# A written work list that reaches to the end of the first FFN group

## The chip, the cores and the metric

The program runs on one core of one Trainium2 chip. The metric is the time of one execution on the device in microseconds (us). The engines in this text are PE (TensorE, matrix products), DVE (VectorE), ACT (ScalarE), POOL (GpSimd) and SP (it issues most transfers). Each engine works through its own queue in order; a row that waits holds up all rows behind it on that engine.

## The reference

```python
# attention: 4 batches, 8 heads, 768 tokens, head size 64; 4 sink keys, window 128
scores = q @ k.T / sqrt(64); keep = is_sink | in_window
a = softmax(where(keep, scores, -1e9)); x = a @ v      # heads side by side: 4 x 768 x 512
# Fourier mix
u = x + real(fft(fft(x, axis=1), axis=2))
# FFN with a normalised input
un = (u - mean(u)) / sqrt(var(u) + 1e-6)
out = u + relu(un @ w_ch1) @ w_ch2                     # 512 -> 2048 -> 512
```

## The kernel before

The 3072 tokens are 24 blocks of 128. The attention walks over them block by block: scores into a double-buffered PSUM tile `s` (L843), a merge and a maximum on DVE (L858, L872), the exponentials on ACT (L883), transposes `pt` (L908), the products with the values `xt` (L944), a transpose back with the sink part added, `x` (L956, L958), and the division on DVE into `us` or `u` (L973). The Fourier mix of a batch, products with constant matrices in two stages (L444, then L471 and L493), runs beside the attention of the next batch; its DVE part splits sums into a high and a low half (L426, L456, L458), combines (L498, L499) and adds into `u` (L509, L510).

The FFN works on six groups of four blocks. Every operand is a pair, a high half rounded by ACT and a low half (a difference) by DVE or POOL, and a product is three products of halves. For an inner tile `f` of 128 columns (sixteen of them), `ch1` (L701, twelve matmuls of 512 columns) makes `h`, `relu` (L749, ACT) the high half, `relu_lo` (L754, DVE) the low half, and `ch2` (L761, twelve matmuls) adds into four accumulators `o`. In the text `h(f)` and `o(f)` are these two sets of twelve matmuls in the first group. The weights arrive as 64-bit pairs of words: three DVE rows join them (L654 to L656, a "join"; number `2f` is the first weight of tile `f`, `2f+1` the second), ACT makes the high half (L684), POOL the low half (L691).

The second group needs, before its first product, for its four blocks: statistics on DVE (L563, L564), a chain of fourteen small DVE steps on a 128x4 tile (L570 to L579), a scaled row block `un` (L587, DVE), four transposes `unt` (L593, PE), and two halves `un_last` (L597 ACT, L602 DVE).

What sets the order: everything up to tile 9 of the first group is called from one string, `WORK`, a letter per call; each letter takes the next call of its kind. This stretch is under the manual schedule, so each engine's queue has the calls in the order of the string. Tiles 10 to 15 of the first group and the second group's preparation (`prepare(1)`) follow in ordinary code without that schedule. There the framework places the rows by its own priorities, and it may put them among the rows of the string where their inputs exist. From the second group on, a loop under the manual schedule sets the order.

```python
for c in WORK or plain:
    other_bank[0] = c
    next(todo[OTHER.get(c, c)])()
```

Of the kernel before, what the change touches and what calls it, by code (L numbers as in the profile page):

```python
# [11 lines left out]
F32 = mybir.dt.float32  # L12
F32R = mybir.dt.float32r
# [6 lines left out]
P = 128  # L20
B, H, S, D = 4, 8, 768, 64
# [32 lines left out]
PREP_N = 4  # L54
# [88 lines left out]
}  # L143
OTHER = {"R": "r", "X": "T", "Y": "T"}
WORK = (
    "TskTsTvqTqTTMTTTTTTTTTTTTTCMfefVsefetifmscvewfqmetiafcRfeswftyViemsvvcGaefwqftemiscoRfeGdtfwyxVmsciq"
    "ueoffweaVzoetmiARscfGnyadewfVoemtivxsVqcufewfeVmiaoetzfRiscVGdyahfweVmtoxvsfcvfuqewdeiamSoetziRfacfy"
    "ewslktoxefufGcsVvqiaezAwfteVoRacdyeswftxViemSuocfsivefawVeqGztmRaciSVyswSxftedGufcmGaesvvfBtwfeqVosc"
    "VaeitzxwmRuycoaVGafedifBTwmeosvqVxitfaVcGfermsnyewztfoucdieafGmseqwvtfBofeVisczTxwmeorufyAidteafcmse"
    "wvqtZhofiTfczewTmeorsfkyiaAleXZxdfTeffTiAdeTZedtuicAswvqzaZofTGeVTftAVXcZGerswydaAoBmitfxTfcewuAsevS"  # L150
    "zTVGqmaDtifTHcfeVrXwyAaeVsHSDxtdTicmHuAfTefwzteosDvvGcaVqirBsmytwfoafcTVHxmeuefsqwVteofaezimsGncahfH"
    "fermvsywxqHteLucfaefotziemsGcaiBLwVrovTyxfdXwAfeTmoeitZisLvqcTAwfefomTeZtiALafudcfeswkzreoLayZisqxvL"
    "TfeLfLdeTLltiALXcZwTLfotAfaeLZTeLdLuLcdiLTwzrsyALoVtGamTcfTfxwtVeuLGeLsvSaAiBzqmTGcVrNwysSCDtfHefTma"
    "eHTfcVsixvteVvwqaOcaAfroqqqqqqemuwTyzoxsfieDtGVHTcTfuemaAwLBToVsGtDafcVieTfvzxHermsNywfedotfaCGmcsie"
    "OHaLBwuvVxtoTcfeHafAzsemNiwfrCdoyfetiOsvcmuewZotLTicfeTfwzeoramyiANfxZtCdacf0OeTwdeoWTiYATZEXdAIWTtA"
    "TcawrZETZYoAWuITyxTAaDEazWIuxTTVEYAPIDVHTVSJSTYAHPzDVVBKuVJVVz1V2VBKVVV2VBVVTVV3jjWYAZAHETZWIYAZEWTA"
    "IPAZEZWITJYAKETWAPIDEVTJIYAKTDPVHAWH2WEITJ2DEKVI2WPHEWI4JKEW2IWEPIWEIPJWEIKE2WJIKEPWIWE2JIKEWIPWEI2J"
    "KEWIWEIEI"
)
# [81 lines left out]
def kernel(  # L241
# [55 lines left out]
    def run(general):  # L297
        tag = "g" if general else ""
        with ExitStack() as p1:
# [463 lines left out]
            def window_attention(fourier, clear, load_constants):  # L763
                with ExitStack() as pa:
# [216 lines left out]
                    with ExitStack() as man:  # L981
# [194 lines left out]
                        def first_group(s):  # L1176
# [9 lines left out]
                            def fourth():  # L1186
                                pf.close()
                                state["pw"] = p1.enter_context(tc.tile_pool(name="wb" + tag, bufs=1))

                            yield s, "second", second  # L1190
                            for f in range(F_LIST):
                                if f > 1:
                                    yield s, "P", lambda f=f: first_product(f)

                                def relu_hi(f=f):
# [4 lines left out]
                                for _ in range(PER_F):  # L1200
# [3 lines left out]
                                    s += 1  # L1204
                                if f < 2 or f > 2:
# [6 lines left out]
                                for i in () if f < 1 else range(4, 8) if f == 1 else range(2 * f + 4, 2 * f + 6):  # L1212
                                    if i == NWA:
# [217 lines left out]
            pw = state.get("pw")  # L1431
            un_last = []
            with (tc.manual_schedule() if MAN0 else ExitStack()):
# [390 lines left out]
```

## Time and profile before

| | |
|---|---|
| median of 3 runs | 742.84 us (741.91 to 743.32) |
| the profiled execution | 742.85 us |
| its span in the trace | 741.1 us |
| PE busy | 721.6 us, 97% of the span |
| DVE busy | 598.8 us, 81% |
| ACT, POOL busy | 344.4 and 180.6 us |

The first product of the second group starts at 303.40 us; the written list covers roughly the first 270 us. A row of the timeline gives start and duration of a piece; square brackets give the idle time of the engine ahead of it and what ended it. Matmuls overlap, so the pitch of a row of them is read from one start to the next.

### The profile page before, as it was taken

To read this page: it belongs to the slowest core of one execution; us is meant where nothing else is said; L and a number is where in the kernel's file an instruction comes from. 1 tells how busy PE (TensorE), PEld (TensorE's weight loads), DVE (VectorE), ACT (ScalarE), POOL (GpSimd) and SP (SyncE) were. 2 spreads that over 40 slices of the span, in tenths; PEclk is the share of its full clock that TensorE was granted. 3 is DMA by queue.
4 is the path that set the end of the run, shared out by engine and by line. 5 is a ranking of instruction groups with operands and counts; after the bars stand their busy time and mean duration, and the time that the engine had idled before them with its cause. 6 is when DMAs were issued, how large, how long until landed. Compare 5 with 4: busy or idle time off the path is not lost.

```text
span 741.1 us, 14738 instructions
## 1 busy us (share of the span) xinstructions
PE 721.6 (97%) x5223; PEld 622.2 (84%) x5223; DVE 598.8 (81%) x1630; ACT 344.4 (46%) x896; POOL 180.6 (24%) x289
## 2 busy tenths in 40 slices
PE   8999999999999999999999999999999999999995
PEld 6677878878787788798988989898989898989895
DVE  7999799899999999597778889587877889564445
ACT  5998678676332333344553333333334233423330
POOL 3686585785344544000000000000000000000002
PEclk9999999999999999999999999999999999999998
DMA  9976245334124653244466566755775657565751
GB/s 249 318 221 188 65 142 157 103 104 169 58 99 171 213 199 115 72 184 157 178 220 237 163 186 221 244 160 174 231 236 170 188 164 241 161 182 164 229 180 61
DMA packets 95306, 129.18 MB, mean 174 GB/s; under 512 B 5956, under 2 KB 60748, under 8 KB 94968
## 3 DMA queue, kind: packets, MB, share of 16 engines
q1 hardware_dynamic: 94216, 124.00, 52.4%
q0 software_dynamic: 720, 3.76, 1.5%
q8 instruction: 43, 0.70, 0.4%
q10 hardware_dynamic: 288, 0.39, 0.1%
q14 instruction: 39, 0.32, 0.1%
HBM read 104.00 MB, written 24.13 MB: 173 GB/s over the span
## 4 chain that ended last, share of the span: by engine, by line
PE 82%; DVE 11%; ACT 3%; issue 1%; DMA 1%; SPq 0%; POOL 0%; DVEq 0%; ACTq 0%
PE h L701 34%; PE p L1535 26%; PE xt L944 4%; PE o L761 4%; PE s L843 3%; PE pt L908 2%; ACT sm L883 1%; PE zb L444 1%; PE za L444 1%; PE x L956 1%; DVE sm L872 1%; PE a L471 1%; DVE s L858 1%; PE zr L444 1%; PE b L493 1%
## 5 line engine op out<-in xcount | busy, mean ns | idle before, releaser
L1535 PE MATMUL p<-w_ring,h_sums 128*128 128x256 f32 x936 | 131.4, 282 | 0.0
L1535 PEld LDWEIGHTS p<-w_ring,h_sums 128*128 128x128 f32 x936 | 123.0, 188 | 3.5 <-DVE u L1367 0.2
L1483 ACT CAST h_sums<-sums 128x256 fp32r<-128x256 f32 (+2 forms) x158 | 89.7, 568 | 68.4 <-PE p L1535 31.1
L1484 DVE TENSOR_TENSOR h_sums<-sums,h_sums 128x256 fp32r<-128x256 f32 (+2 forms) x158 | 98.2, 622 | 17.5 <-ACT h_sums L1483 16.4
L1535 PE MATMUL p<-w2t,h_sums 128*128 128x256 f32 x702 | 110.3, 282 | 0.0
L1557 POOL TENSOR_TENSOR u<-u,u 128x512 f32<-128x512 f32 x3 | 3.8, 1298 | 427.1 <-DVE u L1557 427.1
L1535 PEld LDWEIGHTS p<-w2t,h_sums 128*128 128x128 f32 x702 | 97.6, 189 | 3.4
L701 PE MATMUL h<-un_slots,w 128*128 128x512 f32 x396 | 97.8, 395 | 0.0
L701 PE MATMUL h<-un_last,w 128*128 128x512 f32 x396 | 97.1, 394 | 0.0
L701 PEld LDWEIGHTS h<-un_slots,w 128*128 128x128 f32 x396 | 72.5, 188 | 15.1
L701 PEld LDWEIGHTS h<-un_last,w 128*128 128x128 f32 x396 | 72.2, 188 | 15.0 <-DVE un_slots L602 0.7
L883 ACT ACTIVATE sm<-sm,mx 128x132 f32<-128x132 f32 x192 | 75.8, 399 | 5.1 <-DVE mx L872 4.9
L1697 ACT ACTIVATE sums<-h 128x512 f32<-128x512 f32 x40 | 23.9, 597 | 99.1 <-PE h L701 99.1
L1387 DVE STREAM_TRANSPOSE unf<-un 32x128 f32<-32x128 f32 x192 | 58.1, 302 | 2.8
L1494 DVE TENSOR_TENSOR sums<-sums 128x256 f32<-128x256 f32 x39 | 16.4, 421 | 48.5 <-ACT sums L1697 48.3
L1665 ACT ACTIVATE sums<-h 128x512 f32<-128x512 f32 x40 | 23.9, 598 | 67.7 <-PE h L701 67.7
L872 DVE CUSTOM_DVE_ANT_0 sm<-s,mask 128x132 f32<-128x132 f32 x192 | 45.9, 286 | 3.0 <-DVE s L858 0.5
L944 PE MATMUL xt<-ptl,ldv 128*64 128x128 f32 x384 | 38.0, 284 | 0.0
L843 PE MATMUL s<-ring,q 64*64 64x196 f32 (+1 forms) x640 | 36.3, 340 | 1.6 <-DVE mx L872 1.6
L924 POOL TENSOR_SCALAR_AFFINE_SELECT ptl<-pta 128x512 f32<-128x512 f32 x48 | 32.5, 678 | 19.9 <-ACT pta L915 19.2
L858 DVE COPY_PREDICATED s<-other,s 64x256 f32<-64x256 uint8 x80 | 34.4, 430 | 3.0 <-PE s L843 0.3
L883 ACT ACTIVATION_READ_ACCUMULATOR sm<-sm,mx 128x1 f32 x192 | 36.6, 191 | 0.0
(242 smaller groups left out, 1352.4 us busy)
## 6 DMA issues: line engine op xcount, KB each, us to landing
w_ring<-w2s SPq DMA_DIRECT2D x62, 512.0 KB, 4.4
w2t<-w2s SPq DMA_DIRECT2D x93, 256.0 KB, 3.2
raw<-in_moe_w_ch_dram SPq DMA_DIRECT2D x32, 512.0 KB, 3.2
w2s<-w_ring SPq DMA_DIRECT2D x16, 512.0 KB, 3.3
ldv<-in_v_dram SPq DMA_DIRECT2D x28, 256.0 KB, 2.9
ring<-in_qk_dram SPq DMA_DIRECT2D x24, 264.0 KB, 4.6
w2s<-w2t SPq DMA_DIRECT2D x24, 256.0 KB, 2.5
out_dram<-u SPq DMA_DIRECT2D x22, 256.0 KB, 4.8
```

The lines of the kernel that those rows point to most:

```text
L701: T.matmul(ps[:, :tb], a[:, cs], x[:, :, cc, :], start=n == 0, stop=n == 3 * NCC - 1)
L761: T.matmul(po[i], a[:, ts_], x, start=f == 0 and n == 0, stop=f == NF - 1 and n == 2)
L843: T.matmul(ps[HC * x:HC * x + HC, j, c:c + k.shape[-1]], st["q", g][rows, hp + i, HC * x:HC * x + HC], k, start=True, stop=True)
L858: V.copy_predicated(part(rows, c_out), other[qi > 2][rows], part(rows, c_in))
L872: V.tensor_tensor_reduce(sm[:, h % 4], ps[:, j, c:c + W], mask[min(qi, 3)], -SCALE, 3.0e38, ALU.add, ALU.min, accum_out=mx[:, 0, h:h + 1])
L883: A.activation(sm[:, h % 4], sm[:, h % 4], AF.Exp, bias=mx[:, 0, h:h + 1], scale=-1.0, accum_out=mx[:, 1, h:h + 1])
L924: G.affine_select(lo, a, [[0, 4], [s, P]], compare_op=ALU.is_ge, fill=0.0, base=0, channel_multiplier=-s)
L944: T.matmul(ps[D * j:D * j + D, p, :], st["v", kb(g) - i][:, h, :], a[:, h % 4, :], start=i == 0, stop=i == n - 1)
L1387: V.transpose(unf[32 * q:32 * q + 32, :, r], un[r].rearrange("p (c q j) -> p c q j", c=NCC, q=4)[:, :, q])
L1483: A.copy(hc_hi[:, left(a, n)], src)
L1484: V.tensor_tensor(hc_lo[:, left(a, n)], src, f32(hc_hi[:, left(a, n)]), op=ALU.subtract)
L1535: T.matmul(acc[i][:, 2 * P * tp:2 * P * tp + 2 * P], x, w, start=q == 0 and tp == 0 and n == 0, stop=q == end and n == 2, skip_group_check ...
```

## The change

`F_LIST` (10) goes. The string now also holds tiles 10 to 15 of the first group and the second group's statistics (`p`), scaled rows (`p`), transposes (`b`) and halves (`g`, `Q`), and the opening of the pool that they need (`fifth`). The ordinary loop is left for the general case alone. The string is a new one from its first letters on: rows of the attention and of the Fourier mix have changed places too. The rows themselves are the same on every engine; only their order differs.

```diff
-F_LIST = 10
+    0: "D", 1: "Z", ..., "fourth": "4", "fifth": "5", "p": "p", "b": "b", "g": "g", "Q": "Q", ...
 WORK = (
-    "TskTsTvqTqTTMTTTTTTTTTTTTTCMfefVsefetifmscvewfqmetiafcRfeswftyViemsvvcGaefwqftemiscoRfeGdtfwyxVmsciq"
...
-    "KEWIWEIEI"
+    "TskTTqsTvqTTMCTTTTTTTTTTTTTMfefVsefetifmsvcewfqfetiVsGcmRewafytiefamcsevvwftfeiqmsocRGfxdwyufeVmosqe"
...
+    "PEWpIp2WEJIKEPpWIpWE2IpWEI5PJKEpWIPJKEpWI2pWEIJ2pKEpIWbPgpEQIWbJPgKEQIp2WWEbJ2IgKEQIpPbJ2gKQ"
 )
...
+                            def fifth():
+                                state["pg"].close()
+                                wl = state["wl"] = p1.enter_context(tc.tile_pool(name="wl" + tag, bufs=1))
+                                un_last.append(wl.tile([P, 2, 2, NCC, 2 * P], F32R, name="un_last"))
+                                hc.append(wl.tile([P, 2, len(LEFT) * 2 * P], F32R, name="h_sums"))
+                                hc.append(wl.tile([P, 2, 2 * P], F32R, name="w2t3"))
+                                state[1] = [u_of(*x) for x in groups[1]], [un_last[0][:, :, i] for i in range(2)]
+
+                            def second_group():
+                                blocks = list(enumerate(groups[1]))
+                                for i, x in blocks:
+                                    yield "p", lambda i=i, x=x: stats(*x, u_of(*x), i, groups[1][0])
+                                dev = deviations(*groups[1][0], len(blocks))
+                                for _ in range(14):
+                                    yield "p", lambda: next(dev, None)
+                                for i, x in blocks:
+                                    yield "p", lambda x=x: un_make(*x, u_of(*x))
+                                    yield "b", lambda i=i, x=x: un_turn(*x, banks[1][0].tile([P, 512], F32, tag=banks[1][1], ...))
+                                    yield "g", lambda i=i, x=x: un_hi(*x, state[1][1], i)
+                                    yield "Q", lambda i=i, x=x: un_lo(*x, state[1][1], i)
...
-                            for f in range(F_LIST):
+                            for f in range(NF):
...
+                                if f == PREP:
+                                    yield s, "ch2", lambda: ch2(PREP - 1, hs.pop(PREP - 1), state["po"])
+                                    yield s, "fifth", fifth
...
+                                for _ in range(PREP_N * 2 if f >= PREP else 0):
+                                    x = next(more, None)
+                                    if x:
+                                        yield s, *x
...
-                for f in range(0 if general else F_LIST, NF):
+                for f in range(NF if general else 0):
```

Three places of the order. In the names, the number ahead of the last one is a block, a tile or a part; the last is a serial number that means nothing here.

First, PE where the attention ends. `x_3342` and `x_3332` are the last output block, `h_1` is the first product of tile 1, `o_0` the first accumulator, `ptah` and `ptlh` the halves of tile 0's `h`. Before:

```order
L493 MATMUL b_2_3307<-cst,zb_2_3170 128x258
L701 MATMUL h_1_3318<-un_slots,w_ring 128x512 x12
L956 MATMUL x_3342<-ident,xs_3250 128x128 x4
L958 MATMUL x_3342<-vs_1964,skt_3201 128x512
L761 MATMUL o_0_3362<-w_ring,ptah_3300 128x512 x2
L761 MATMUL o_0_3362<-w_ring,ptlh_3301 128x512
```

Now:

```order
L492 MATMUL b_2_3321<-cst,zb_2_3164 128x258
L959 MATMUL x_3332<-ident,xs_3317 128x128 x4
L961 MATMUL x_3332<-vs_1968,skt_3190 128x512
L700 MATMUL h_1_3341<-un_slots,w_ring 128x512 x12
L764 MATMUL o_0_3365<-w_ring,ptah_3289 128x512 x2
L764 MATMUL o_0_3365<-w_ring,ptlh_3290 128x512
```

The last output block now stands ahead of `h(1)` and no longer directly ahead of `o(0)`.

Second, DVE in the first tiles of the FFN. `stat` is the 128x4 tile of the second group's chain, `cv`, `cw` and `w2r` are what joins write, `zr` is a low half of the last Fourier mix. Before, at joins 5 and 6:

```order
L654 TENSOR_SCALAR w2r_3470<-raw_3189 128x512
L564 BN_AGGR stat_4_4040<-bn_1_4050 128x2
L655 SCALAR_TENSOR_TENSOR w2r_3470<-raw_3189,w2r_3470 128x512
L570 TENSOR_SCALAR stat_4_4040<-stat_4_4040 128x4
L656 SCALAR_TENSOR_TENSOR w2r_3470<-raw_3189,w2r_3470 128x512
L456 TENSOR_TENSOR zr<-zr_3_3458,zr 1x386
L654 TENSOR_SCALAR cv_3491<-raw_3241 128x512
L572 TENSOR_SCALAR stat_4_4040<-stat_4_4040 128x4
L655 SCALAR_TENSOR_TENSOR cv_3491<-raw_3241,cv_3491 128x512
```

Now the chain's first two steps stand here, at joins 14 and 15 and the low half of `h(6)`:

```order
L653 TENSOR_SCALAR cw_3800<-raw_3725 128x512
L654 SCALAR_TENSOR_TENSOR cw_3800<-raw_3725,cw_3800 128x512
L655 SCALAR_TENSOR_TENSOR cv_3799<-raw_3725,cw_3800 128x512
L569 TENSOR_SCALAR stat_4_2306<-stat_4_2306 128x4
L653 TENSOR_SCALAR cw_3823<-raw_3762 128x512
L654 SCALAR_TENSOR_TENSOR cw_3823<-raw_3762,cw_3823 128x512
L655 SCALAR_TENSOR_TENSOR w2r_3792<-raw_3762,cw_3823 128x512
L757 SCALAR_TENSOR_TENSOR h_0_6_3844<-h_6_3807,h_0_6_3843 128x512
L571 TENSOR_SCALAR stat_4_2306<-stat_4_2306 128x4
```

The chain's other twelve steps follow one by one between the joins up to number 27, and the first two scaled rows, which stood after the low half of `h(2)` and ahead of that of `h(5)`, now stand behind the low half of `h(12)` and behind join 28. On PE the first block's transposes, which stood between `h(5)` and `o(5)`, stand behind `o(11)`, so that `o(5)` follows `h(5)` directly; `h(12)` stands ahead of `o(10)`.

Third, PE in the attention, at the second score group of block 5 (`s_2_673`, `s_2_661`) and the transposes `pt_1` of block 4. Before:

```order
L944 MATMUL xt_600<-pta_3_516,ldv_293 64x128 x2
L908 MATMUL pt_1_663<-ident,sm_0_583 128x128 x4
L843 MATMUL s_2_673<-ring,q_391 64x196
L843 MATMUL s_2_673<-ring,q_391 64x200
L843 MATMUL s_2_673<-ring,q_391 64x196
```

Now:

```order
L947 MATMUL xt_623<-pta_3_534,ldv_291 64x128 x2
L846 MATMUL s_2_661<-ring,q_402 64x196
L846 MATMUL s_2_661<-ring,q_402 64x200
L846 MATMUL s_2_661<-ring,q_402 64x196
L846 MATMUL s_2_661<-ring,q_402 64x200
L846 MATMUL s_2_661<-ring,q_402 64x196
L846 MATMUL s_2_661<-ring,q_402 64x200
L846 MATMUL s_2_661<-ring,q_402 64x196
L846 MATMUL s_2_661<-ring,q_402 64x200
L911 MATMUL pt_1_676<-ident,sm_0_587 128x128 x4
```

The four transposes have moved behind the scores. Moves of this kind, by one or two rows, are found in most blocks.

## Rows read from the trace of the kernel before

**Rows 1.** The page, part 1: busy time of each engine, its share of the span, and its instructions.

```profile
PE 721.6 (97%) x5223; PEld 622.2 (84%) x5223; DVE 598.8 (81%) x1630; ACT 344.4 (46%) x896; POOL 180.6 (24%) x289
```

**Rows 2.** Stretches of the whole program: length, then busy time and instructions of PE, PEld (weight loads), DVE, ACT and POOL, the granted PE clock as a share of full speed, the share of the DMA engines, GB/s.

```profile
100.00:150.00 50.00, 49.98 (x572) 39.97 (x570) 46.13 (x188) 38.00 (x141) 36.18 (x67) 1.00 0.47 138
...
200.00:250.00 50.00, 45.80 (x222) 38.17 (x221) 48.50 (x89) 14.38 (x28) 21.68 (x18) 0.97 0.40 137
...
650.00:700.00 50.00, 50.00 (x314) 44.99 (x313) 25.86 (x49) 17.41 (x30) 0.00 (x0) 1.00 0.59 180
```

**Rows 3.** Timeline of PE from the end of the attention to the second group: start, duration, row, and in brackets the idle time ahead with what ended it. `unt` are the second group's transposes.

```profile
199.17 0.70 PE L761 MATMUL o<-w_ring,ptah 128*128 128x512 f32 x2 [1.26 <-DVE us L973]
...
209.26 0.62 PE L444 MATMUL zr<-cst,gh 128*128 128x386 f32 x2 [0.80 <-DVE za L458]
...
213.23 0.62 PE L444 MATMUL zb<-cst,gh 128*128 128x386 f32 x2 [0.36 <-DVE zr L456]
...
224.91 0.95 PE L471 MATMUL a<-cst,za 128*128 128x258 f32 x6 [1.73 <-DVE d L499]
...
239.21 2.89 PE L701 MATMUL h<-un_slots,w 128*128 128x512 f32 x12
241.94 0.60 PE L593 MATMUL unt<-ident,un 128*128 128x128 f32 x4
242.78 0.50 PE L761 MATMUL o<-w2t,h 128*128 128x512 f32 x1 [0.25 <-ACT h L749]
243.95 0.49 PE L761 MATMUL o<-w2t,h 128*128 128x512 f32 x1 [0.67 <-POOL w2t L691]
244.84 4.14 PE L761 MATMUL o<-w2t,h 128*128 128x512 f32 x10 [0.39 <-DVE h L754]
248.82 0.63 PE L701 MATMUL h<-un_slots,w_gh 128*128 128x512 f32 x2
...
254.32 2.90 PE L761 MATMUL o<-w_ring,h 128*128 128x512 f32 x12
257.06 0.62 PE L701 MATMUL h<-un_slots,w_gh 128*128 128x512 f32 x2
...
303.40 2.97 PE L701 MATMUL h<-un_last,w_ring 128*128 128x512 f32 x12
```

**Rows 4.** Stretches of 1 us around tile 5: length, PE busy time and instructions, the granted PE clock (1.00 is 2.4 GHz, 0.50 is 1.2 GHz), DMA.

```profile
245.00:246.00 1.00, 1.00 (x4) 0.60 0.63 254
246.00:247.00 1.00, 1.00 (x4) 0.50 0.00 0
247.00:248.00 1.00, 1.00 (x4) 0.50 0.00 0
248.00:249.00 1.00, 1.00 (x4) 0.69 0.87 287
```

**Rows 5.** Timeline of DVE in the same part: `bn` and `stat` are the second group's statistics and chain, `un` its scaled rows, `za` and `d` rows of the last Fourier mix, `h` and `h_sums` the low halves of `h(5)` and `h(10)`, `cv` the last row of join 14.

```profile
206.20 0.68 DVE L563 BATCH_NORM_STATS2 bn<-u 128x6 f32<-128x512 f32 x1
...
208.66 0.55 DVE L458 TENSOR_TENSOR za<-za,za 128x386 fp32r<-128x386 f32 x1
...
211.31 0.70 DVE L570 TENSOR_SCALAR stat<-stat 128x4 f32<-128x4 f32 x1
...
213.94 1.26 DVE L572 TENSOR_SCALAR stat<-stat 128x4 int32<-128x4 int32 x1
...
224.02 0.42 DVE L498 TENSOR_TENSOR d<-asb,b 128x257 f32<-128x257 f32 x1
...
242.69 1.49 DVE L587 TENSOR_SCALAR un<-u,stat 128x512 f32<-128x512 f32 x1
244.11 0.68 DVE L754 SCALAR_TENSOR_TENSOR h<-h,h 128x512 fp32r<-128x512 f32 x1
...
248.62 0.69 DVE L656 SCALAR_TENSOR_TENSOR cv<-raw,cw 128x512 int32<-128x512 int32 x1
...
274.56 0.69 DVE L754 SCALAR_TENSOR_TENSOR h_sums<-h,h_sums 128x512 fp32r<-128x512 f32 x1 [1.08 <-ACT h_sums L749]
```

**Rows 6.** DVE rows that read or write `stat` (chain, aggregates, scaled rows) in two stretches: length, busy time and instructions.

```profile
205.00:246.00 41.00, 7.05 (x18) 0.99 0.45 154
246.00:304.00 58.00, 2.00 (x2) 0.98 0.46 155
```

**Rows 7.** Timeline of ACT: the high half of `h(5)` and that of join 14.

```profile
242.13 0.60 ACT L749 ACTIVATE h<-h 128x512 fp32r<-128x512 f32 x1 [1.49 <-PE h L701]
...
249.34 0.62 ACT L684 CAST w_gh<-cv 128x512 fp32r<-128x512 f32 x1 [1.57 <-DVE cv L656]
```

**Rows 8.** Timeline of POOL: two low halves of weights, the second that of join 14.

```profile
213.69 1.48 POOL L691 TENSOR_TENSOR w2t<-w2r,w2t 128x512 fp32r<-128x512 f32 x1
...
250.03 1.30 POOL L691 TENSOR_TENSOR w_gl<-cv,w_gh 128x512 fp32r<-128x512 f32 x1 [0.90 <-ACT w_gh L684]
```

**Rows 9.** Timeline of PE in the attention: four transposes, and the score group of `s_2_673` that follows them.

```profile
32.06 0.66 PE L908 MATMUL pt<-ident,sm 128*128 128x128 f32 x4
33.24 0.91 PE L843 MATMUL s<-ring,q 64*64 64x196 f32 x16 [0.52 <-DVE mx L872]
```

**Rows 10.** Waits of PE from 14 to 199 us: row, what it waited for, us in total, times, longest.

```profile
PE s L843 <- DVE mx L872: 1.6, 4, 0.6
PE pt L908 <- ACT sm L883: 0.8, 2, 0.6
```

More of the change, by code (lines that the diff above doesn't have):

```diff
@@ L151 @@
[L151 to L155, printed above, removed]
@@ new lines @@
+    "czsixmweRuoyVtGacfedaifBwTmeoVxGsvqtfeVacifezwsnmrouGyfetdiafcmBswqveVoTxfefitzscmuAwefodrayieftmesv"
+    "qciZahfwefoTzxmeTlitfAXdcZewTfdeoTAdirZTyskAuZftefTzcTVGesVvqAtXwfefsoZaAiemGTficfewdrXyoAteDsSHBamq"
+    "iTHfcvfxtAwueTezsSGDaViTmcHrfXyAVetwsDaVHqfemsvcGfvxtfwemuocadieszqwBrdoaVyTGxVtuciafeVwtfezsnomacHh"
+    "frefwvHsyqxmteLucoafGeftizBwmscaoeViTLxvwfXfoAmeiTeZrsLvqyiATfefmteTZciLuwAftoezskadfeLaZcLifTLwxfeL"
+    "doTLerdXLlyiAtZTcLpswvqAtLfoeTfZTesLpuAiLmazTLcVGTfrsfyetVwqemaAoSLXicvfxLGtfeTDwseSLdHuLBaizTHmcNAr"
@@ new lines @@
+    "sVywCtfqeVTGVaqqqqqqcvDvGxtOwTcfuoemrHsyBzafiteVGTcfaVAsxwTemuoDtwLaofTVcifeazHemNxwfrsvCdoayfeGOemH"
+    "tBLucisVtwfTcHefazAsemoNvxifedwrafCmosyeivOtiZLucfTewfzoTemiNAftCZacOeTwdxof0TedWiXArTyZEtdATIWcTwrY"
+    "ATaAZEYZoWuITyaAtzxWTcEuwYTaDEVPoAVIVSSHTJzYVaIDBTxVTAHuDPVVVz1JVVBK2VVVKV2BVVVTVHpYApZ3jjWTAZAWYEIZ"
+    "EWTAIPAZEZWITJYAKETWAPIDEVTJHYAKTDI2VAHWPWETJI2DEKWI2VEIPWJH4EK2WIWEPIpEWIPJKEpWI2JKEpWIPpWEI2JpWEIK"
+    "PEpWIp2WEJIKEPpWIpWE2IpWEI5PJKEpWIPJKEpWI2pWEIJ2pKEpIWbPgpEQIWbJPgKEQIp2WWEbJ2IgKEQIpPbJ2gKQ"
@@ L709, in open_ffn, with u_of @@
                     load_w(i)
+            def u_of(b, blk):
+                return U[b if b in U else b - 1][:, blk, :]
             def start_ffn(s):
@@ L1188, in fourth @@
                                 state["pw"] = p1.enter_context(tc.tile_pool(name="wb" + tag, bufs=1))
+                            def fifth():
[14 more added lines that the diff above has]
+                                    yield "p", lambda x=x: un_make(*x, u_of(*x))
+                                    yield "b", lambda i=i, x=x: un_turn(*x, banks[1][0].tile([P, 512], F32, tag=banks[1][1], name=f"unt_1_{i}", bufs=1))
+                                    yield "g", lambda i=i, x=x: un_hi(*x, state[1][1], i)
+                                    yield "Q", lambda i=i, x=x: un_lo(*x, state[1][1], i)
+                            more = second_group()
                             yield s, "second", second
-                            for f in range(F_LIST):
+                            for f in range(NF):
                                 if f > 1:
                                     yield s, "P", lambda f=f: first_product(f)
+                                if f == PREP:
+                                    yield s, "ch2", lambda: ch2(PREP - 1, hs.pop(PREP - 1), state["po"])
+                                    yield s, "fifth", fifth
                                 def relu_hi(f=f):
@@ L1204, in first_group @@
                                     s += 1
-                                if f < 2 or f > 2:
+                                if f < 2 or f > 2 and f != PREP:
                                     j = f if f < 2 else f - 1
@@ L1211, in first_group @@
                                         yield s, "keep", lambda j=j: keep_w2(j)
-                                for i in () if f < 1 else range(4, 8) if f == 1 else range(2 * f + 4, 2 * f + 6):
+                                for i in () if f < 1 else range(4, 8) if f == 1 else range(2 * f + 4, min(2 * f + 6, 2 * NF)):
                                     if i == NWA:
@@ L1223, in first_group @@
                                     yield s, "I", lambda i=i: join_lo(i)
+                                for _ in range(PREP_N * 2 if f >= PREP else 0):
+                                    x = next(more, None)
+                                    if x:
+                                        yield s, *x
+                            for op, fn in more:
+                                yield s, op, fn
                             assert not ev
@@ L1431, in run @@
             pw = state.get("pw")
-            un_last = []
+            steps, wl = iter(()), state.get("wl")
             with (tc.manual_schedule() if MAN0 else ExitStack()):
```

12 lines of the change are left out of this document (3 added, 9 removed), and 2 rows, old and new, of the table CODES.

## The prediction

> **What bounds the kernel now.** I read the busy times first [rows 1]: PE works 721.6 of 741.1 us. At most 19.5 us are open to an order of rows that leaves the work as it is. Then the stretches [rows 2]: late in the program PE is busy for all 50.00 of 50 us, so nothing is to be had there. PE gaps remain in the stretch of the list: 150 to 250 us has 47.75 and 45.80 busy, and between 200 and 250 us DVE, at 48.50, is as full as PE. The granted clock there is 0.97 on average, so some PE time is slow time as well. Third, PE's timeline from 199 to 303 us [rows 3] names each gap and who ended it, and DVE's timeline [rows 5] shows what stood ahead of the row that PE waited for. From 254.32 us on the rows of twelve matmuls that are shown carry no bracket: PE waits for nothing, and the second group starts at 303.40. So I count what each gap before that point becomes. Whatever PE gains by 303 us reaches the end whole, since behind it PE is the bound.
>
> One set of twelve matmuls takes 2.74 us (254.32 to 257.06 [rows 3]); the sums below use this.
>
> **Part 1: the last output block ahead of h(1).** `o(0)` now waits 1.26 us for the division of that block on DVE [rows 3]. With `h(1)` between the block's products and `o(0)`, 2.74 us of PE work cover that wait. Gain 1.26. If the block's products waited themselves in their new place, part of it would come back; I see no wait at them before.
>
> **Part 2: the chain leaves the last Fourier mix.** DVE rows on `stat` take 7.05 us between 205 and 246 us, in 18 rows [rows 6]: two aggregates, two scaled rows, fourteen chain steps. The steps shown cost 0.70 and 1.26 us [rows 5] though they touch 128x4 numbers; one scaled row costs 1.49. Beside the chain I count each PE wait with what leaves ahead of it:
> - `zr` waits 0.80 for the low half `za` (row at 208.66 [rows 5]). A join goes behind it, and its rows are of 0.7 us (248.62 [rows 5]); gone with that wait: 0.80.
> - `zb` waits 0.36 for `zr`'s low half; the chain row of 0.70 at 211.31 stood ahead of it. Gain 0.36.
> - `a` waits 1.73 for `d` (224.02 [rows 5]). Two chain rows alone, 0.70 and 1.26, are 1.96. Gain 1.73; the statistics rows (0.68 each [rows 5]) stay where they are and are not counted.
>
> Sum of this part 2.89. The weak point is that joins and low halves fill the places that come free; the lower bound is half of it, 1.45.
>
> **Part 3: o(5) directly behind h(5).** From 241.94, when the first transposes start, to 248.82, when `h(6)` starts, are 6.88 us [rows 3]. The work in it is 2.74 for `o(5)` and the four transposes, which are only moved. Their row lasts 0.60, but the end of a row holds the drain of the pipeline: one matmul lasts 0.50 at 242.78, where the pitch is 2.74 / 12 = 0.23. So the transposes are 0.60 - 0.27 = 0.33 us of work. So 6.88 - 2.74 - 0.33 = 3.81 us are lost. Part of it is three waits (0.25, 0.67 and 0.39), part the clock: the four rows of 1 us give 0.60, 0.50, 0.50 and 0.69 [rows 4], which is 1.71 us of full-speed work lost, and they follow right behind the three waits. The waits come from a scaled row: DVE's `un` of 1.49 us at 242.69 [rows 5] stands ahead of `h(5)`'s low half at 244.11. It is moved to behind `h(12)`. Now `o(5)` can start when ACT's high half is done. `h(5)`'s stream ended at 241.94; ACT's row began at 242.13 and took 0.60 [rows 7], and `o(5)` began at 242.78, so 0.84 us pass. Two matmuls later it needs the low half, 0.68 long, which costs about 0.25 more. Waits that remain 1.09, gain 3.81 - 1.09 = 2.72. This takes it that the clock stays at 1.00; a rival below does not.
>
> DVE's scaled row at 242.69 runs beside POOL's weight halves, and the chain row of 1.26 us at 213.94 ends with POOL's 1.48 us row at 213.69 [rows 5, 8]; the other step, 0.70 long, did not. So such rows are two prices: 0.70 alone, 1.26 beside POOL. The Trainium skill ("SBUF — State Buffer", section "Who interferes with whom") says that DVE and GpSimd share one pair of ports as an exclusive lock, which rows of this kind can take, and that the loser blocks fully. The trace agrees as far as the 1.26 us row goes. By that rule the moved rows would meet POOL's halves in their new places too, since there is one for every join; this speaks against the change, and a rival prices it from rows.
>
> **Part 4: what the moved rows cost in their new place.** The scaled rows and the chain go to where DVE is the bound. From the end of `h(5)`'s low half (244.11 + 0.68 = 244.79, called T) DVE runs joins back to back: six rows to the end of join 14 at 249.31 [rows 5], 0.75 each. Its weight then goes through ACT (249.34, 0.62 [rows 7]) and POOL (250.03, 1.30 [rows 8]), ready at 251.33, T + 6.54. Before, PE began `h(6)` at 248.82, T + 4.03. Now it begins 2.74 - 0.46 = 2.28 after T (two of `o(5)`'s matmuls, 0.23 each, are behind it by then). `h(7)`, which follows `h(6)`, asks for that weight at its third matmul, T + 2.28 + 2.74 + 0.46 = T + 5.48. It waits 1.06. So one part of what part 3 frees is met again as a wait for a weight. On top come fourteen chain steps and the two scaled rows: 7.05 is the sum with two small aggregates, so nearly 7 us of DVE time at the old prices. Each chain step of the string stands between two joins, and a tile of PE work is 5.5 us against six joins of 0.72 and a low half of 0.68, 5.0 us of DVE: 0.5 us free per tile, in eight tiles 4. DVE's first idle time of any size comes at 274.56 (1.08 [rows 5]). Bounds: below, only the 1.06 and no more (1.0); above, 1.06 plus what does not fit, 7 - 4 = 3, less a part that the idle time at 274.56 takes in, near 3.5 in total. I take 2.1, about the middle, since neither end has a row that it lies on.
>
> **Part 5: the new order in the attention.** Score groups are now often called ahead of the transposes of the block before. In the third place of the order, the group had waited 0.52 us for DVE's maximum, behind transposes of 0.66 [rows 9]; without them it would wait about 0.52 + 0.6 = 1.1, and the transposes run later at no cost. All such waits of PE in the attention are small: 1.6 us in four for scores, 0.8 in two for `pt` [rows 10]. So the best that can happen is that about 1.5 of them go, and a bad case is four times 0.6, 2.5. I take a loss of 0.6, one such swap.
>
> **The sum.** 1.26 + 2.89 + 2.72 = 6.87 gained, 2.1 + 0.6 = 2.7 lost: 4.2 net. The profiled execution has 742.85 us for a span of 741.1, and the median of the runs is the same to 0.01, so the same difference holds for both: 742.85 - 4.2 = 738.65, given as **738.6 us**. A measurement of this kernel can tell about 0.2%, 1.5 us, from no change.
>
> **The rivals.**
> - The clock falls again. It fell behind three waits of together 1.31 us within 2.1 us [rows 3, 4]; 1.09 remain at `o(5)` and 1.06 at `h(7)`. If so, the 1.71 us come back: 740.3. For it: the waits are nearly as long; against it: other waits (1.26, 1.73) had no drop that lowers the 0.97 of the stretch further. Chance 0.20.
> - DVE takes what it is given. If the scaled rows and steps meet POOL's rows at 1.26 and 1.49 us [rows 5], part 4 costs 3.5 or more and part 2 gives half: 4.2 - 1.4 - 1.4 = 1.4 net, 741.4; halfway, 740.0. For it: joins stand back to back from 244.79 to 274. Chance 0.15.
> - It goes better. Part 4 costs 1.0 and 1.5 us of attention waits go: 4.2 + 1.1 + 2.1 = 7.4, so 735.5. Chance 0.15.
> - Slower. Scores called sooner wait for the two score buffers, which DVE frees. A wait is 1.6 / 4 = 0.4 us [rows 10], and the gain without part 5 is 4.8; with 12 more such waits in the 48 groups nothing is left, and with 18 (7.2 us) it ends at 742.85 - 4.8 + 7.2 = 745.2. For it: DVE is busy 46.13 of 50 us in this stretch [rows 2]; against it: PE is busy 49.98 of 50 there, so with the old order it hardly waits, and most moves are of one or two rows. Chance 0.05.
> - The rows may not stand where the string says. The order on DVE shows the scaled rows behind `h(12)`'s low half, so no chance is left for it.
>
> **How the numbers follow.** The forecast has 0.45, within about 1.5 us of 738.6; the rivals have 0.20, 0.15, 0.15 and 0.05. The range is 735.5 to 741.6: its lower end is about the better case, its upper the DVE case at its full price, and about 2 in 10 lie outside. Faster by over 0.2% means below 741.4: forecast, clock and better case nearly whole and a part of the DVE case, 0.83. Within 0.2%: the rest of the DVE case and a weak form of the slower one, 0.11. Slower by over 0.2%: 0.06.
>
> **What would show it.** Right: the second group's first product at about 299 instead of 303.40; no wait of 1.26 at the first `o`, none near 1.73 at `a`; `o(5)` directly behind `h(5)` with about 1.1 us of waits and a clock of 1.00 in the next 4 us; a wait of about 1 us for POOL's low half at `h(7)`; DVE busy over 95% from 245 to 275. Wrong: clock rows of 0.50 at tile 5; waits of PE in the attention summing to more than 6 us; several waits for POOL or DVE between 245 and 300; or gaps after 300 us, where I count on none.

## The result, and the profile after

The changed kernel takes 748.27 us (median of 4 runs) against 742.48 us before: a ratio of 1.0072, 95% interval 1.0054 to 1.0089. Run again it took 746.73 against 742.29 us, 1.0068 (1.0051 to 1.0084). Forecast were 738.6 us and 735.5 to 741.6; the sign was wrong too. One of the 4 runs, the profiled one, was disturbed (3951 us; the ratio leaves it out), so all rows of after are from the second measurement. Its profiled execution took 746.12 us, span 744.3. It is the shortest of its four, so the rows show 3.2 us of the 4.4 between the medians.

PE's timeline of the changed kernel, with the rows that answer to [rows 3] (line numbers are shifted by up to 3), and the wait that has no counterpart there:

```profile
45.93 0.91 PE L846 MATMUL s<-ring,q 64*64 64x196 f32 x16 [2.96 <-DVE mx L875]
...
201.29 0.62 PE L764 MATMUL o<-w_ring,ptah 128*128 128x512 f32 x2
202.61 0.50 PE L764 MATMUL o<-w_ring,ptlh 128*128 128x512 f32 x1 [0.70 <-DVE ptlh L757]
...
213.46 0.62 PE L443 MATMUL zb<-cst,gh 128*128 128x386 f32 x2 [0.22 <-DVE za L457]
...
216.86 0.62 PE L443 MATMUL zb<-cst,gh 128*128 128x386 f32 x2 [1.54 <-DVE zr L455]
...
227.63 0.97 PE L470 MATMUL a<-cst,za 128*128 128x258 f32 x6 [1.00 <-DVE d L498]
...
241.83 2.88 PE L700 MATMUL h<-un_slots,w 128*128 128x512 f32 x12
245.40 3.29 PE L764 MATMUL o<-w2t,h 128*128 128x512 f32 x12 [0.69 <-ACT h L752]
248.52 0.62 PE L700 MATMUL h<-un_slots,w_gh 128*128 128x512 f32 x2
...
251.91 0.74 PE L700 MATMUL h<-un_slots,w_gh 128*128 128x512 f32 x2 [0.48 <-ACT w_gh L683]
253.28 0.50 PE L700 MATMUL h<-un_slots,w_gl 128*128 128x512 f32 x1 [0.63 <-POOL w_gl L690]
...
255.67 2.88 PE L764 MATMUL o<-w_ring,h 128*128 128x512 f32 x12
...
264.86 2.61 PE L700 MATMUL h<-un_slots,w 128*128 128x512 f32 x10 [0.36 <-POOL w L690]
...
279.27 2.60 PE L700 MATMUL h<-un_slots,w 128*128 128x512 f32 x10 [0.20 <-POOL w L690]
...
303.51 0.63 PE L592 MATMUL unt<-ident,un 128*128 128x128 f32 x4 [0.57 <-DVE un L586]
...
306.79 2.97 PE L700 MATMUL h<-un_last,w_ring 128*128 128x512 f32 x12
```

The second group starts at 306.79 and not at 303.40 [rows 3], 3.39 us later; the span is 3.2 longer. So nothing is lost behind that point. Three anchors that both kernels have split it (start of `o(0)`, of `h(5)` and of the second group):

| stretch | before | after | measured | forecast |
|---|---|---|---|---|
| to `o(0)` | 199.17 | 201.29 | +2.12 | -1.26 + 0.6 = -0.66 |
| `o(0)` to `h(5)` | 40.04 | 40.54 | +0.50 | -2.89 |
| `h(5)` to the second group | 64.19 | 64.96 | +0.77 | -2.72 + 2.1 = -0.62 |

All three went the other way than forecast. The first is one wait of 2.96 us early in the attention and what follows it. In stretches of 1 us of the changed kernel (columns as in [rows 4]) the granted clock falls to half behind that wait:

```profile
46.00:47.00 1.00, 1.00 (x20) 0.69 (x22) 1.00 (x2) 1.00 (x7) 1.00 (x1) 0.99 0.06 16
47.00:48.00 1.00, 1.00 (x14) 1.00 (x12) 0.97 (x2) 0.39 (x1) 1.00 (x2) 0.50 0.00 0
48.00:49.00 1.00, 1.00 (x9) 0.67 (x6) 0.83 (x2) 0.32 (x1) 0.86 (x3) 0.50 0.03 8
49.00:50.00 1.00, 1.00 (x6) 0.91 (x6) 0.96 (x9) 0.54 (x2) 0.00 (x0) 0.50 0.14 30
50.00:51.00 1.00, 1.00 (x9) 0.92 (x7) 0.94 (x3) 1.00 (x5) 0.62 (x2) 0.80 0.98 268
```

That is 0.50 + 0.50 + 0.50 + 0.20 and 0.01, 1.71 us of full-speed work. Who made PE wait stands in the timelines of POOL, SP's queue and DVE:

```profile
36.45 0.58 POOL L322 DMA_DIRECT2D cst<-in_dft_dram  x1
...
36.49 0.63 SPq L806 DMA_DIRECT2D ring<-in_k_mid_dram  x1
37.22 0.52 SPq L371 DMA_DIRECT2D xr<-x0d  x1
...
43.73 0.41 DVE L374 TENSOR_TENSOR xr<-xr 4x255 f32<-4x255 f32 x1 [4.24 <-DMA xr<-x0d]
```

`xr` is a row tile of 8 KB. DVE waits 4.24 us for it, and the maxima behind it on DVE are what PE's scores wait for. In the kernel before the order was the other way round, and DVE did not wait (its row has no bracket):

```profile
37.41 0.32 SPq L372 DMA_DIRECT2D xr<-x0d  x1
37.77 0.55 SPq L803 DMA_DIRECT2D ring<-in_k_mid_dram  x1
...
38.60 0.57 POOL L323 DMA_DIRECT2D cst<-in_dft_dram  x1
...
40.10 0.41 DVE L375 TENSOR_TENSOR xr<-xr 4x255 f32<-4x255 f32 x1
```

The new string calls two large loads, 837 KB of constants on POOL and 264 KB of keys on SP, so early that both are issued ahead of that small one. The forecast never looked at these two queues there.

### The profile page after: what moved, and what is told of

Same layout as the page of the kernel before. It is cut to its first block, busy times and chain, and to the rows that moved or that the text cites. A ratio compares the mean times of both kernels' runs of the same rounds, so it can differ in the third digit from the quotient of the medians.

```text
span 3949.8 us, 14729 instructions
## 1 busy us (share of the span) xinstructions
PE 3940.8 (100%) x5223; PEld 3064.9 (78%) x5223; DVE 604.1 (15%) x1630; ACT 347.0 (9%) x896; POOL 173.3 (4%) x289
## 4 chain that ended last, share of the span: by engine, by line
PE 100%; POOL 0%; ACT 0%; issue 0%; DVE 0%; POOLq 0%
PE h L700 39%; PE p L1565 27%; PE o L764 6%; PE xt L947 6%; PE s L846 4%; PE pt L911 3%; PE za L443 2%; PE zb L443 2%; PE x L959 2%; PE a L470 2%; PE b L492 1%; PE zr L443 1%; PE x L961 1%; PE d L1677 1%; PE warm L1041 1%; PE s L840 1%
## 5 line engine op out<-in xcount | busy, mean ns | idle before, releaser
L1565 PEld LDWEIGHTS p<-w_ring,h_sums 128*128 128x128 f32 x936 | 659.6, 926 | 31.8 <-issue 31.8
L1565 PE MATMUL p<-w_ring,h_sums 128*128 128x256 f32 x936 | 661.9, 1031 | 0.0
L1565 PEld LDWEIGHTS p<-w2t,h_sums 128*128 128x128 f32 x702 | 517.5, 932 | 32.7 <-issue 32.7
L700 PE MATMUL h<-un_slots,w 128*128 128x512 f32 x396 | 536.0, 1694 | 0.0
L700 PE MATMUL h<-un_last,w 128*128 128x512 f32 x396 | 535.8, 1694 | 0.0
L1565 PE MATMUL p<-w2t,h_sums 128*128 128x256 f32 x702 | 526.1, 1037 | 0.0
L700 PEld LDWEIGHTS h<-un_slots,w 128*128 128x128 f32 x396 | 354.8, 913 | 140.8 <-issue 140.8
L700 PEld LDWEIGHTS h<-un_last,w 128*128 128x128 f32 x396 | 355.0, 919 | 134.9 <-issue 134.9
L846 PE MATMUL s<-ring,q 64*64 64x200 f32 (+1 forms) x640 | 171.9, 1324 | 0.0
L911 PE MATMUL pt<-ident,sm 128*128 128x128 f32 x192 | 139.6, 1053 | 0.0
```

Of the source, the lines that this page charges most:

```text
L700: T.matmul(ps[:, :tb], a[:, cs], x[:, :, cc, :], start=n == 0, stop=n == 3 * NCC - 1)
L846: T.matmul(ps[HC * x:HC * x + HC, j, c:c + k.shape[-1]], st["q", g][rows, hp + i, HC * x:HC * x + HC], k, start=True, stop=True)
L911: T.transpose(ps[:, j], sm[:, j, :P], ident)
L1565: T.matmul(acc[i][:, 2 * P * tp:2 * P * tp + 2 * P], x, w, start=q == 0 and tp == 0 and n == 0, stop=q == end and n == 2, skip_group_check ...
```

## The experiments

**The two halves apart.** Two theories stood against each other. Theory A: the new order of the attention costs. Theory B: the tail costs, because joins come late behind chain steps and scaled rows. First the new order up to the letter that opens the FFN's second pool, with the old tail; then the old order up to there, with the new tail. The two edits are given in words, since a string is cut at one letter in each.

```diff
-WORK = old
+WORK = new up to the first "1", then what is left of old
```

> The kernel before with the new order of the string up to the end of the attention alone (the letters up to the one that opens the FFN's second pool); behind it the order before, with tiles 10 to 15 and the second group's preparation in ordinary code. Theory A: 748 to 753 us. Theory B: 742 to 743 us, no slower than before.

746.58 us, 1.0059 (1.0043 to 1.0076). The attention alone is the larger part.

```diff
-WORK = new
+WORK = old up to the first "1", then what is left of new
```

> The changed kernel with the order of the kernel before up to the same letter, and the new order behind it. Theory A: 737 to 740 us. Theory B: 747 to 749 us.

745.27 us, 1.0041 (1.0026 to 1.0055): the tail loses as well. So neither theory holds alone. The two losses, 4.3 and 3.0 us, do not add up to the whole of 4.4: where the old attention meets the new tail, PE waits 1.26 and 1.29 us in `o(0)`, and in the changed kernel 0.70. The changed kernel, unaltered, was run beside them. It has one long wait in the attention and no gain in the tail, but neither theory's sum: PE's waits from 14 to 199 us are 5.3 us (theory A said 8 or more), those from 245 to 305 us 2.9 (theory B said 7 or more).

> The changed kernel once more, unaltered, for a trace of an ordinary execution. Both theories expect about 748 us. Theory A (the new order in the attention costs): the second group's first product comes late already at the end of the attention, PE's waits from 14 to 199 us sum to 8 us or more (3.6 before), and the tail behind 200 us gains about 4 us. Theory B (the tail costs): PE's waits in the attention stay near 3.6 us, and between 245 and 305 us PE waits 7 us or more, for joins that come behind chain steps and scaled rows.

**The old string with the rest in code order.**

```diff
-CUT, MAN0 = 97, False
+CUT, MAN0 = 97, True
```

> The kernel before, its string untouched, with tiles 10 to 15 and the second group's preparation in the order of their code under the manual schedule, so that the chain and the scaled rows stand behind tile 9 and not ahead of it. Theory A: 738 to 741 us, since the rows leave the last Fourier mix and the attention keeps its order. Theory B: 746 us or more, since the chain and the scaled rows meet the joins late, one behind the other.

762.33 us, 1.0268 (1.0251 to 1.0285). Theory B's mechanism is real when nothing spreads the rows: PE waits for two scaled rows at the end of the group. This is its table of PE's waits from 199 to 330 us (row, waited for, us in total, times, longest):

```profile
PE unt L593 <- DVE un L587: 15.8, 2, 10.8
```

**Which load.** The keys' letter `k` behind `xr`'s letter `S`:

```diff
-umcieswktzeoSfRaGdyefialceswf
+umcieswtzeoSfRaGdyefialkceswf
```

> The changed kernel with one letter moved: the load of the batch's middle keys (264 KB) is issued behind the load of the 8 KB row tile xr and no longer ahead of it, as in the kernel before. Theory L (a small transfer is queued behind a large one, and DVE waits for it): the wait of 2.96 us on PE and the 3 to 4 us of half clock behind it go, 4 to 5 us less than the changed kernel, 742 to 743 us. Rival O (the new order of scores and transposes costs, the transfer is only what DVE happens to wait for): less than 1.5 us change, 745 us or more.

747.79 us, 1.0062 (1.0042 to 1.0082), and DVE still waits 3.54 us for `xr`. Theory L (a small transfer is held up by a large one issued ahead of it) fell for the keys alone. DVE's row fourteen letters later:

```diff
-tfxiVeoufcRdsyAwztefoa
+tfxieoufcRdsyAwzteVfoa
```

> The changed kernel with the loads as they are, but DVE's row that reads xr is called fifteen letters later, so that scores, maxima and a division stand ahead of it. Theory L: DVE has other work until the transfer has landed, the wait goes as well, 742 to 743 us. Rival O: 745 us or more.

746.48 us, 1.0046 (1.0029 to 1.0062). The wait only changed engine: an ACT row that reads `xr` too now waited 4.79 us, and PE 4.09 us. The opposite edit of the kernel before, `k` ahead of `S`:

```diff
-qewdeiamSoetziRfacfyewslktoxef
+qewdkeiamSoetziRfacfyewsltoxef
```

> The kernel before with the load of the middle keys moved ahead of the load of xr, as the change has it; nothing else differs. Theory L: DVE waits some 3 to 4 us for xr, 745.5 to 747 us. Rival O: 742 to 743 us.

743.1 us, 1.0008 (0.9999 to 1.0018): a wait of 0.67 us on DVE and nothing on PE. So the keys are not the one that counts. The constants' fifth load, letter `G`, stands behind `S` in both strings, but POOL may come to it sooner than SP to `S`. It was called later in the changed kernel, then sooner in the kernel before, where it was issued at 35.36 us, ahead of `xr` at 37.51:

```diff
-tzeoSfRaGdyefialceswfqvtfxiVeou
+tzeoSfRadyefialceswfqvtfxiVGeou
```

> The changed kernel with one letter moved: the fifth load of constants, 837 KB on POOL's queue, is issued behind the load of the row tile xr as in the kernel before, and no longer ahead of it. Theory G (that load fills the DMA engines ahead of the 8 KB of xr): xr lands within 3 us of its issue and not after 6.5, PE's wait of 2.96 us and the half clock behind it go, 742 to 743 us. Rival O (order of scores and transposes): still 745 us or more.

745.38 us, 1.0040 (1.0026 to 1.0055); `xr` lands earlier, DVE's wait is 1.79 us.

```diff
-deiamSoetziRfacfyewslktoxefufGcs
+deiamSoetGziRfacfyewslktoxefufcs
```

> The kernel before with that load of constants called ahead of where the change has it, so that it is issued ahead of xr; nothing else moves. Theory G: DVE waits 3 to 5 us for xr, 745 to 747 us. Rival O: 742 to 743 us.

744.71 us, 1.0031 (1.0020 to 1.0043). This one letter costs the kernel before 2.3 us, with DVE waiting 2.01 us for `xr`. So theory G (the load of constants holds `xr` up) holds in its direction, but both runs fell short of its forecasts: e9 was to end at 743 us or less, e10 at 745 or more with a wait of 3 to 5 us. Both letters back:

> The changed kernel with both loads back behind xr: the constants' fifth load and the middle keys. Theory G+L (xr, 8 KB, is held up by whatever large load is issued just ahead of it): xr lands within 3 us, DVE waits for it less than 0.5 us, no PE wait over 1 us between 40 and 60 us and no half clock there; 742 to 744 us, where the rest over 741 is the tail's. Rival O: waits of 1 us and more for ACT and DVE stay at 50 to 55 us as with one load moved, 745 us.

745.25 us, 1.0031 (1.0018 to 1.0045): 2.7 us above the kernel before, where the changed kernel is 4.4 above it. DVE waits only 0.66 us (theory G+L said less than 0.5), and yet PE waits some us later; this is PE's timeline of that run:

```profile
51.61 0.66 PE L911 MATMUL pt<-ident,sm 128*128 128x128 f32 x4 [1.16 <-ACT pta L918]
53.05 1.44 PE L846 MATMUL s<-ring,q 64*64 64x196 f32 x16 [0.78 <-DVE mx L875]
```

Behind these two waits the clock again loses 1.71 us, and `o(0)` starts at 201.43, as late as with the loads early (201.29); but this trace is of the longest of the run's five executions (746.21 us) and that of the changed kernel of its shortest. The late transfer had covered a second fault: in the new order of these letters the maxima reach ACT too late (its row at 50.21 us waits 1.40 for one), and ACT's copy behind it reaches PE too late. Rival O (the order of scores and transposes costs) was right to that extent. One row of DVE that stands ahead of the next maxima is a long one, beside a row of POOL:

```profile
50.04 1.27 POOL L409 TENSOR_TENSOR f<-u 128x512 f32<-128x512 f32 x1 [0.43 <-DVE u L976]
...
50.30 1.55 DVE L409 TENSOR_TENSOR f<-u 128x512 f32<-128x512 f32 x1
```

The nearest such row of the kernel before, at 48.15, takes 0.69. Where the loss lies was found by putting back the old first 260 letters, then only the first 170 (with all large loads early):

> The changed kernel with the order of the kernel before for the first 260 letters (some 60 us), the new one behind them. If all that the attention loses is lost there, the time is that of the changed kernel less 3 to 4.5 us, 742 to 743.5 us; if the new order loses all through the attention, 745 us or more.

741.69 us, 0.9987 (0.9978 to 0.9997).

> The changed kernel with the order of the kernel before for the first 170 letters only (some 32 us), so that both loads stand ahead of xr. If the stretch from letter 170 to 260 carries the loss, 745.5 to 747 us; if the first 170 letters carry it, 742 to 743 us.

746.11 us, 1.0052 (1.0037 to 1.0067). So letters 170 to 260, some 32 to 60 us, carry 4.4 us (746.11 against 741.69), as much as the whole loss; with the old ones there the changed kernel is 0.8 us faster than before. The traces give the account by stretches. With the old start `o(0)` begins at 197.14 and not at 201.29, so the new order of the first 260 letters costs 4.15 us. The new order behind them gains 2.03 (197.14 against 199.17), and the tail loses 0.50 + 0.77 = 1.27. No run took away single rows in letters 170 to 260, so which of them make the 1.16 and 0.78 us is not shown.

**Why o(0) waited.** In the kernel before, `h(1)` is called behind the last output block; then, besides, this block's division is called earlier on DVE:

```diff
-HPzDVVBKuVJVVz1
+HzDVVBKuPVJVVz1
```

> The kernel before with h(1) called behind the last output block, which is the first of the three places alone. If the term of 1.26 us is right, 741.0 us; if DVE ahead of o(0) or the rows behind it wait in its place, 742.3 us as before.

742.56 us, 1.0002 (0.9993 to 1.0011). `o(0)` waits 1.26 us at the same time as before, though the block's products start 2.8 us earlier (194.28 against 197.08). DVE's timeline of this run shows what stood ahead of the division (`us`):

```profile
196.76 0.68 DVE L426 TENSOR_TENSOR gl<-f,gh 128x512 fp32r<-128x512 f32 x1
197.35 0.68 DVE L410 TENSOR_TENSOR f<-us,us 128x512 f32<-128x512 f32 x1
197.96 0.41 DVE L420 TENSOR_TENSOR f<-f 128x255 f32<-128x255 f32 x1
198.29 0.68 DVE L973 TENSOR_TENSOR us<-x,mx 128x512 f32<-128x512 f32 x1
```

No row has a bracket: the division waited for its turn on DVE, not for PE.

```diff
-HPzDVVBKuVJVVz1
+HzDVVBKuPzVJVV1
```

> The kernel before with h(1) behind the last output block, as in the run with that alone, and with this block's division and a few of its neighbours called earlier on DVE. Theory Q (o(0) waits for the division because of the rows queued ahead of it on DVE, not for its inputs): the wait of 1.26 us goes, 741.2 us, or 742.3 us if the Fourier rows that are now behind it take it back at zr and a. If the wait is one for the block's products, it stays.

742.82 us, 1.0002 (0.9993 to 1.0011). The wait at `o(0)` is gone, and `zr`, which waited 0.80 us [rows 3], now waits

```profile
209.79 0.62 PE L444 MATMUL zr<-cst,gh 128*128 128x386 f32 x2 [2.43 <-DVE za L458]
```

1.63 more. DVE is the bound in this stretch (48.50 of 50 us busy [rows 2]), and this order of its rows moved PE's wait without shrinking it.

**What a chain row costs.** The prediction read the steps' durations as their cost. Theory P says that most of it is a wait for POOL, which passes to the next row when the step is gone. Nine of fourteen steps are left out of the kernel before, for the second group and the groups behind it; then all of the chain and the scaled rows leave the stretch, with its order kept (old order to tile 5, new from there).

```diff
-                for _ in range(4):
+                for _ in range(4 if (b, blk) == (0, 0) else 1):
```

> The kernel before with nine of the fourteen chain steps of the second group left out (three of the four Newton iterations of its standard deviations). Theory P (most of a chain row's time in the last Fourier mix is a wait for POOL, which passes to the next row when the step is gone): PE's waits at zr, zb and a still sum to over 2.3 us (2.89 before), 742 us. The prediction's reading (the steps cost their rows' time): the wait of 1.73 us at a falls below 0.8, about 741 us.

742.74 us, 1.0003 (0.9993 to 1.0013); waits at `zr`, `zb` and `a` of 0.8, 0.3 and 1.6, 2.7 together where 2.89 stood.

> The order of the kernel before up to tile 5 of the FFN (without the second group's chain and scaled rows), the changed kernel's order from tile 5 on, statistics at their old place. The prediction's reading of the chain: waits at zr, zb and a fall from 2.89 to below 1.5 us. Theory P: they stay above 2.3 us. From tile 5 on both expect the changed kernel's 65 us to the second group, 0.8 more than before. 741.5 us by the first, 743 by the second.

743.53 us, 1.0013 (1.0003 to 1.0022). PE's timeline of that run:

```profile
210.12 0.62 PE L443 MATMUL zr<-cst,gh 128*128 128x386 f32 x2 [1.54 <-DVE za L457]
...
214.02 0.62 PE L443 MATMUL zb<-cst,gh 128*128 128x386 f32 x2 [0.29 <-DVE zr L455]
...
225.17 0.95 PE L470 MATMUL a<-cst,za 128*128 128x258 f32 x6 [1.39 <-DVE d L498]
```

3.22 us together, against 2.89 with the chain in between. The chain's time did not come free; rows of the joins took it. Where the kernel before has its step of 1.26 us at 213.94, this run has a row of a join:

```profile
214.85 1.67 DVE L654 SCALAR_TENSOR_TENSOR cv<-raw,cv 128x512 int32<-128x512 int32 x1
```

The step of 0.70 us at 211.31 [rows 5] is no other case: it ends at 212.01, and a row of POOL that had begun before it ends at 211.97. A step that starts while POOL is idle is short. Both rows are from the kernel before:

```profile
210.80 1.17 POOL L510 TENSOR_TENSOR u<-u,d 128x255 f32<-128x255 f32 x1
...
215.72 0.15 DVE L575 SCALAR_TENSOR_TENSOR stat<-stat 128x4 f32<-128x4 f32 x1
```

In their new places, in the changed kernel, the two steps of 0.70 and 1.26 us take 0.17 and 0.16; the one behind them, at 257.17, meets a row of POOL there and takes 1.26. The rows of the changed kernel where DVE and POOL meet show how the time passes on:

```profile
214.40 1.28 POOL L690 TENSOR_TENSOR w<-cv,w 128x512 fp32r<-128x512 f32 x1 [3.90 <-issue]
...
214.50 1.73 DVE L655 SCALAR_TENSOR_TENSOR w2r<-raw,w2r 128x512 int32<-128x512 int32 x1
```

Other rows of this kind take 0.69 us; this one started 0.10 behind POOL's and lasted 1.04 longer. To take POOL away, ACT copied the second halves of joins 4 to 13. The subtraction is left out, so these are no low halves; the run is there for its times:

```diff
+                if 4 <= i < NWA:
+                    A.copy(d[1], state.pop(("t", i)).bitcast(F32))
+                    return
                 G.tensor_tensor(d[1], state.pop(("t", i)).bitcast(F32), f32(d[0]), op=ALU.subtract)
```

> The changed kernel with the second halves of the weights of joins 4 to 13 made by an ACT copy and not by POOL's subtraction, so they are not low halves any more: POOL reads nothing while these joins run. Theory P: every row of these joins takes 0.42 or 0.69 us, none 1.5 us or more, PE's waits at zb and a (1.54 and 1.00 us) fall by 1.5 us or more together. If the long rows are DVE's own, they stay.

744.3 us, 2.4 less than the changed kernel. Its trace is of its shortest execution, 742.32 us. Groups of DVE's join rows from 209 to 249 us (count, busy us, mean ns, idle ahead), first of the changed kernel, then of this run:

```profile
L654 DVE SCALAR_TENSOR_TENSOR cv<-raw,cv 128x512 int32<-128x512 int32 x5 | 6.4, 1276 | 0.2
L653 DVE TENSOR_SCALAR w2r<-raw 128x512 int32<-128x512 int32 x5 | 5.3, 1065 | 0.0
L655 DVE SCALAR_TENSOR_TENSOR w2r<-raw,w2r 128x512 int32<-128x512 int32 x5 | 4.5, 899 | 0.2
```

```profile
L654 DVE SCALAR_TENSOR_TENSOR cv<-raw,cv 128x512 int32<-128x512 int32 x5 | 3.5, 693 | 0.2
L653 DVE TENSOR_SCALAR w2r<-raw 128x512 int32<-128x512 int32 x5 | 2.6, 525 | 0.0
L655 DVE SCALAR_TENSOR_TENSOR w2r<-raw,w2r 128x512 int32<-128x512 int32 x5 | 3.5, 693 | 0.2
```

The long rows are gone (the longest of these is 0.96); from `o(0)` to `h(5)` this run takes 239.37 - 201.09 = 38.28 us, 2.26 less. PE's waits there fall to 0.72 at `ptlh`, 0.17 and 0.52 at `zb`, and none at `a`.

**A version that beats both.** The kernel before with the new order of the attention from letter 260 on, and nothing else.

```diff
-WORK = old
+WORK = old to letter 260, then new up to the first "1", then what is left of old
```

> The kernel before with the new order of the attention between letter 260 and the opening of the FFN's second pool alone; start and tail as before. The new order there brings the last output block's end about 2 us earlier (197.14 us at o(0) against 199.17). If the tail hands that on, 740 to 741 us; if DVE, which bounds the Fourier mix, takes it back at o(0) and zr, 742.4 us.

741.24 us, 0.9983 (0.9974 to 0.9992). `o(0)` starts at 197.47 and the second group at 301.78, 1.7 and 1.6 us earlier than before.

## Why the prediction was wrong

**Part 5 failed by what it left out.** It weighed swaps of scores and transposes and put -1.5 to +2.5 us on them. The stretch to `o(0)` lost 2.12 us, and 2.12 + 1.26 = 3.4 with the wait that was there before, where 0.6 stood. Of a row moved in such a string every queue counts: loads of 837 and 264 KB were called ahead of one of 8 KB, DVE waited 4.24 us for that, PE 2.96, and the clock took 1.71. The rival "slower" had the right sign and place, with the wrong mechanism: not many short waits for score buffers but one long one for a transfer. That the loads alone cured only 1.7 of 4.4 us (e13) shows a second weakness of the new order in the same 90 letters, which is shown as a place and not explained row by row.

**Part 1 failed at its cover.** It let 2.74 us of PE work hide a wait for a DVE row, and did not ask what that row waited for. It waited for its turn on DVE: in e8 its inputs were there 2.8 us sooner and the 1.26 us stayed where they were, and e15 turned them into 1.63 at `zr`. In the changed kernel, where DVE's order differs too, `o(0)` waits 0.70 for a low half instead.

**Part 2 failed at its price.** It read 0.70 and 1.26 us as costs of chain steps. They were mostly the time in which DVE waited for POOL, which the next row pays when the step is gone (e11, e16, e12). The changed kernel waits 0.22 + 1.54 + 1.00 = 2.76 us at `zb` and `a` and nothing at `zr`, where 2.89 were to go. The two prices in part 3, 0.70 alone and 1.26 beside POOL, are misread: both steps end with a row of POOL, and a step by itself takes 0.15 to 0.17. They were used as a rival for the new place only; in the old place they should have taken the gain away. The Trainium skill ("SBUF — State Buffer", section "Who interferes with whom") says that a DVE row with two SBUF inputs contends with a GpSimd row that reads SBUF, and that the later of the two blocks; the 1.73 us row agrees.

**Part 3 came out in its place and could not be kept.** The waits came out as forecast (0.69 at `o(5)` and a row that lasts 0.4 longer than 2.90, against 1.09) and the clock stayed at 1.00 there. From `h(5)` to `h(6)` are 248.52 - 241.83 = 6.69 us where 9.61 stood; without the 0.33 of transposes that only moved, the gain is 2.59 (forecast 2.72). But e8, with the same rows there as before, had no fall of the clock either and needed 303.10 - 239.11 = 63.99 us from `h(5)` to the second group, against 64.19 with it. So the 1.71 us of the clock were hardly a gain to be had: PE at full clock waits 0.62 us for join 14's low half instead. The kernel before shows the same by itself. Of its 97 executions beside the experiments, 30 have the mean granted clock of the profiled one, 0.995, and a median of 742.68 us; 57 have 0.997 or 0.998 (e8, without the fall, has 0.997) and 742.39, only 0.3 us less.

**Part 4 was right in mechanism and too small.** `h(7)` waits 0.48 + 0.63 = 1.11 us (forecast 1.06), and with 0.36, 0.20 and 0.57 later the brackets hold 2.24 (forecast 2.1). But a wait costs more than its bracket: `h(6)` and `h(7)` together take 255.67 - 248.52 = 7.15 us, 1.67 more than twice 2.74. From `h(6)` to the second group are 306.79 - 248.52 = 58.27 us, 3.69 more than the 54.58 before, and 3.36 without the transposes that moved behind it. That is near the upper bound of 3.5 and takes back all of part 3. DVE was busy 28.05 of 30 us from 245 to 275, 94% where over 95% stood.

That gains before 303 us reach the end whole holds for the changed kernel: from the second group's start to the end of the span are 437.7 us before and 437.5 after. It does not hold for every change: in e11 the second group starts at 302.02, 1.38 earlier, and 438.7 us follow; why was not looked into.

## What to carry to other kernels

When a list of calls is written anew, compare the order on every queue, the DMA issuers first, and follow each small transfer that a busy engine reads: ask which large load is now issued ahead of it. Where one engine is the bound, a wait that names it may only move when the waiting engine's work (e8) or the bound engine's own rows (e15) change places. A row's time in the trace is not its work if another engine's row holds it up: look for rows of two engines that end together, and compare with the same row elsewhere. Here taking the held-up rows away gained nothing (e11, e16), and taking away the rows that held them up gained 2.26 us between `o(0)` and `h(5)` (e12).

## What the runs showed of the hardware

An 8 KB transfer issued 0.8 us behind an 837 KB one on POOL's queue, and 0.7 us behind a 264 KB one on its own, landed about 6.5 us after its issue (37.22 to 43.73). With the 264 KB one behind it it took 5.8 us (e5), with the 837 KB one behind it 4.0 (e9), with both behind it 3.3 (e13). In the kernel before, with the 837 KB one issued 1.2 us behind it, DVE's row found it there at 40.10, at most 2.7 us after the issue.

A DVE step on 128x4 numbers takes 0.15 to 0.17 us by itself; in the kernel before the three of the second group's chain that started during a row of POOL took 0.59, 0.70 and 1.26 us and ended within 0.04 us of that row's end.

When the clock fell behind short waits, it cost about the same each time (1.71 us at tile 5 before, behind the wait of 2.96, and in e13 behind 1.16 and 0.78), at different places. Behind the wait of 10.76 us in e4 it was at half until 300 us, more than 5 us after PE had started again at 294.92. In e18 waits of 1.56, 1.15 and 0.78 us were followed by no fall, so waits of this length do not settle it alone.
